# Dummy matmuls in the TensorE gaps of a planned attention and two-layer kernel

## The chip, the cores and the metric

One core of a Trainium2 chip runs the whole kernel. The metric is the device time of one execution in microseconds (us); lower is better. All times here are from three timed runs or from one profiled execution.

## The reference

Inputs: `q`, `k`, `v` of shape (4, 8, 576, 64) in float32, a scalar `tau`, and two pairs of weights, (512, 2048) and (2048, 512).

```python
scores = (q @ k.T) / sqrt(64)                       # per batch and head, 576 x 576
scores = where(scores >= max(scores, -1) - tau, scores, -1e9)
attn = exp(scores - max(scores, -1)); attn /= sum(attn, -1) + 1e-9
x = (attn @ v)                                      # heads side by side: 2304 x 512
h = x @ moe_w_in;  g = where(h >= 1, h, where(h <= -1, 0, (h + 1)**2 / 4)); x = g @ moe_w_out
h = x @ moe2_w_in; g = h - tanh(h);                 out = g @ moe2_w_out
```

## The kernel before

The attention is cut into 144 units of 128 query rows. A unit is a chain over four engines: `u_qk` (TensorE, PE) writes scores of 128 x 576 into a PSUM tile; `u_max` (VectorE, DVE) reads them for the row maximum; `u_exp` (ScalarE, ACT) reads them for the exponential; `u_mask` (DVE) reads them once more, compares them with the threshold and sums; then the rows are split in two halves of 16 bits, transposed and multiplied with `v`.

The scores lie in `s_ts[0]`, `s_ts[1]`, `s_ts[2]`. Each is one PSUM tile of 128 x 2 x 512 floats, so of two banks, and a unit uses columns 0 to 287 of both. The first 32 units (`N0`) take two or three of the tiles in turn. From then on every unit uses `s_ts[0]`, and the halves of the other two are the four accumulators `acc_ts` of the two feed-forward layers. Those layers run in 160 steps beside the units: `m_h` (matmuls into a tile `ph`), `m_act`, `m_dve`, `m_split`, `m_out` (matmuls into the accumulators) and, at the end of a layer, `m_evac`, which copies the accumulators out with ACT and DVE, one half tile after the other.

Every operation is first recorded by `Program.add` with an estimated duration. `Program.issue` then plays the program through as a list scheduler: each engine takes the ready operation of least `prio`, and `Program.run` gives its start and end. The instructions are emitted in the order of these planned starts, all engines in one list; the semaphores that order conflicting accesses of a tile are put in by the framework from that list. The planner's own dependences (`box`, `apart`) are finer: they compare the byte ranges.

`run` models the PE with two speeds: an operation takes `o.dur` when `self.warm` holds, else twice that. `run` also has a branch for fillers. It needs `self.filler`, which is set only when `FILL` holds, after all operations are recorded and before they are planned:

```python
out = s_ts[0][:, 1, HALF:512]
P.fill_bank = out.tensor.name, 1
P.filler = lambda: nc.tensor.matmul(out=out, lhsT=half_word[:, 0:128], rhs=half_word[:, 0:224], start=True, stop=True)
```

`half_word` is the float32 identity read as bf16. The output is columns 288 to 511 of the second bank of `s_ts[0]`, next to the scores. A planned operation carries the number of fillers in `o.fill`; `issue` emits them on the PE just ahead of it, unless an accumulation in that bank is open. Fillers are not operations of the plan, and nothing in the plan waits for them.

Of the kernel before, what the change touches and what calls it, by code (L numbers as in the profile page):

```python
# [46 lines left out]
LATENCY = {"PE": 55, "DVE": 34, "ACT": 34, "POOL": 78, "SP": 30}  # L47
DRAIN = 163
PATIENCE = 3.0
FILL = False  # L50
WINDOW = 3413.33
DIRECT = (3,)
NARROW = (0, 1)
# [109 lines left out]
class Program:  # L163
# [65 lines left out]
    def run(self, o, t):  # L229

        e = o.eng
        if e == "SP":
            turn = o.dur > 1000
            begin = max(self.dma, t + (1000 if turn else 900))
            self.dma = begin + o.serve
            self.free[e] = max(t + o.dur, begin - (2000 if turn else 4500)) + 60
            return t, self.dma + 1250
        if e == "PE":
            load, f0, f1 = self.load, self.free[e], t - 250
            fill = 0  # L240
            if self.filler and f0 > 6000 and t - f0 > 400:
                fill = int((f1 - f0) / 96)
                for k in range(int(f0 / WINDOW), int(f1 / WINDOW) + 1):
                    load[k] = load.get(k, 0.0) + max(min(f1, (k + 1) * WINDOW) - max(f0, k * WINDOW), 0.0)
            while self.slot < int(t / WINDOW):
                self.warm = load.get(self.slot, 0.0) > (0.4 if self.warm else 0.8) * WINDOW
                self.slot += 1
            d = o.dur * (1 if self.warm else 2)
            k = int(t / WINDOW)
            load[k] = load.get(k, 0.0) + min(t + d, (k + 1) * WINDOW) - t  # L250
            load[k + 1] = load.get(k + 1, 0.0) + max(t + d - (k + 1) * WINDOW, 0.0)
            self.free[e] = t + d
            o.fill = fill
            return t, t + d + DRAIN
        if o.lock:
            t = max(t, self.lock)
            self.lock = t + o.dur - OVERLAP[e]
        self.free[e] = t + o.dur - OVERLAP[e]
        return t, t + o.dur
# [73 lines left out]
def attention_moe_moe2(ctx: ExitStack, tc: tile.TileContext, qd, kd, vd, tau, w1, w2, ident, out):  # L333
# [711 lines left out]
    for k, _, fn, a in sorted(agenda, key=lambda e: e[:2]):  # L1045
# [3 lines left out]
        fn(*a)  # L1049
    if FILL:  # L1050
        half_word = idt.bitcast(BF16)
# [53 lines left out]
```

## Time and profile before

| | before |
|---|---|
| median of 3 runs | 1085.52 us (1084.07 to 1090.26) |
| the profiled execution, its own time | 1084.37 us |
| its span, first to last instruction | 1082.6 us |
| PE busy, instructions | 1030.0 us (95%), 5826 |
| DVE, ACT, POOL busy | 629.2, 632.4, 504.0 us |
| mean granted TensorE clock | 0.987 |

The busy time of the PE is made of matmuls whose ends are modelled, so it is not PE at its peak. The granted clock is a share of full speed: 1.00 is 2.4 GHz and 0.50 is 1.2 GHz.

### The profile page before, as it was taken

Reading aid. Unit: us, or ns where it says so; the run is one execution under the profiler, and the core shown is the slowest. Engines: PE = TensorE matmul, PEld = TensorE weight load, DVE = VectorE, ACT = ScalarE, POOL = GpSimd, SP = SyncE. Lnnn points to the kernel's source line nnn. Section 1 sums busy time; section 2 is a strip of 40 time slices with the busy share of each in tenths; the row PEclk is TensorE's granted clock in tenths of the full one; section 3 lists DMA queues with packets and bytes.
Section 4 is the critical chain, followed back from the end, with each engine's and each line's share of the span. In section 5 each row is a group of like instructions: output and inputs, shape, how many; then the busy total and the mean of one; then the engine's idle time right before and its main releaser. Section 6 shows DMA issues by size and latency. Waiting matters only on the chain.

```text
span 1082.6 us, 17257 instructions
## 1 busy us (share of the span) xinstructions
PE 1030.0 (95%) x5826; PEld 831.0 (77%) x5826; DVE 629.2 (58%) x1380; ACT 632.4 (58%) x1158; POOL 504.0 (47%) x510
## 2 busy tenths in 40 slices
PE   5789999999999999999999999999999999998997
PEld 3567777767777788778888888778877878888986
DVE  5987978898898766674347665742253331113432
ACT  5778777768776777676457777764353332222332
POOL 3654778768686555445345555444333212220000
PEclk8999999999999999999999999999999999999999
DMA  6999999999999998889679988897586655557997
GB/s 148 176 229 335 313 319 320 297 275 353 352 336 314 315 243 231 226 227 232 209 206 277 266 212 217 211 230 207 171 269 194 178 189 183 188 193 285 369 343 248
DMA packets 231384, 272.93 MB, mean 252 GB/s; under 512 B 170240, under 2 KB 170368, under 8 KB 231296
## 3 DMA queue, kind: packets, MB, share of 16 engines
q1 hardware_dynamic: 231296, 271.83, 86.5%
q8 instruction: 46, 0.75, 0.3%
q14 instruction: 42, 0.34, 0.1%
HBM read 193.40 MB, written 38.27 MB: 214 GB/s over the span
## 4 chain that ended last, share of the span: by engine, by line
PE 70%; DVE 12%; ACT 8%; DMA 5%; issue 4%; POOL 1%; SPq 0%; ACTq 0%; DVEq 0%; POOLq 0%
PE ph L354 35%; PE s L354 35%; DVE small L354 3%; DMA w<-in_w_dram 2%; ACT e L354 2%; DVE wr L354 2%; DVE e L354 2%; DMA vr<-in_vd_dram 2%; DVE g L354 1%; DVE xw L354 1%; ACT a L354 1%; DVE ph L354 1%; DMA wo<-wf0o 1%; ACT top L354 1%; DMA at<-w 1%
## 5 line engine op out<-in xcount | busy, mean ns | idle before, releaser
L354 PE MATMUL ph<-xh,wi 128*128 128x512 f32 x1024 | 271.1, 399 | 4.0 <-DVE g L354 3.7
L354 POOL TENSOR_TENSOR a<-e,a 128x512 f16<-128x512 f32 x236 | 180.9, 785 | 188.9 <-ACT a L354 172.4
L354 POOL TENSOR_TENSOR gl<-g,gh 128x512 fp32r<-128x512 f32 x114 | 152.3, 1336 | 199.1 <-ACT gh L354 179.4
L354 PEld LDWEIGHTS ph<-xh,wi 128*128 128x128 f32 x1024 | 188.0, 189 | 45.4 <-DVE g L354 6.2
L354 PE MATMUL s<-gh,wo 128*128 128x512 f32 (+1 forms) x640 | 157.4, 377 | 5.2 <-ACT gh L354 1.9
L354 PE MATMUL s<-wo,gh 128*128 128x512 f32 x576 | 155.1, 398 | 1.1 <-ACT w L354 0.7
L354 PE MATMUL ph<-xl,wi 128*128 128x512 f32 x512 | 144.8, 396 | 0.2 <-DVE xl L354 0.2
L354 DVE SCALAR_TENSOR_TENSOR e<-s,small,e 128x576 f32<-128x576 f32 x129 | 104.8, 813 | 67.1 <-ACT small L354 66.4
L354 DVE TENSOR_REDUCE small<-s 128x1 f32<-128x576 f32 x144 | 108.2, 752 | 47.7 <-PE s L354 46.8
L354 ACT ACTIVATE gh<-g 128x512 fp32r<-128x512 f32 (+1 forms) x152 | 88.2, 581 | 78.5 <-DVE g L354 76.2
L354 DVE TENSOR_TENSOR g<-ph,t 128x512 f32<-128x512 f32 (+1 forms) x80 | 50.8, 635 | 142.2 <-ACT t L354 138.9
L354 PEld LDWEIGHTS s<-gh,wo 128*128 128x128 f32 x640 | 112.0, 191 | 26.4 <-ACT gh L354 4.2
L354 PEld LDWEIGHTS s<-wo,gh 128*128 128x128 f32 x576 | 105.2, 188 | 22.9 <-ACT gh L354 1.1
L354 ACT ACTIVATE e<-s,small 128x576 f32<-128x576 f32 x129 | 94.9, 736 | 44.6 <-DVE small L354 41.7
L354 ACT ACTIVATE t<-ph 128x512 f32<-128x512 f32 (+1 forms) x80 | 44.1, 552 | 120.6 <-PE ph L354 120.4
L354 PEld LDWEIGHTS ph<-xl,wi 128*128 128x128 f32 x512 | 95.9, 188 | 23.2 <-DVE xl L354 1.2
L354 PE MATMUL s<-gl,wo 128*128 128x512 f32 (+1 forms) x320 | 89.4, 381 | 4.5 <-ACT xh L354 2.1
L354 DVE TENSOR_TENSOR ph<-ph,t 128x512 f32<-128x512 f32 (+1 forms) x80 | 51.4, 643 | 70.1 <-ACT t L354 69.2
L354 ACT ACTIVATE t<-ph,small 128x512 f32<-128x512 f32 (+1 forms) x80 | 51.4, 642 | 66.4 <-PE ph L354 66.2
L354 ACT ACTIVATE a<-e 128x576 f16<-128x576 f32 x118 | 80.1, 679 | 6.8 <-DVE e L354 4.8
L354 PE MATMUL s<-wo,gl 128*128 128x512 f32 x288 | 82.3, 393 | 1.0 <-ACT w L354 1.0
L354 PEld LDWEIGHTS s<-gl,wo 128*128 128x128 f32 x320 | 57.6, 190 | 15.8 <-ACT xh L354 3.4
(107 smaller groups left out, 1513.6 us busy)
## 6 DMA issues: line engine op xcount, KB each, us to landing
w<-in_w_dram SPq DMA_DIRECT2D x64, 512.0 KB, 6.0
wi<-wf0i SPq DMA_DIRECT2D x64, 512.0 KB, 4.1
wo<-wf0o SPq DMA_DIRECT2D x64, 512.0 KB, 4.3
wi<-wf1i SPq DMA_DIRECT2D x64, 512.0 KB, 3.8
wo<-wf1o SPq DMA_DIRECT2D x64, 512.0 KB, 3.7
kr<-in_kd_dram SPq DMA_DIRECT2D x32, 288.0 KB, 4.4
wf0i<-wi SPq DMA_DIRECT2D x16, 512.0 KB, 6.1
wf0o<-wo SPq DMA_DIRECT2D x16, 512.0 KB, 5.6
```

Source lines behind the costliest of these rows:

```text
L354: P.add(eng, dur, lambda: fn(**kw), outs, ins, serve, lock, load)
```

## The change

`FILL` becomes true. With the other edits, the planner gives a filler count to each PE operation before which its plan has the PE idle by more than 250 ns, from 3 us of planned time on: one filler for each 96 ns of the gap but its last 100 ns. The lines that counted fillers as activity in the planner's model of the clock go, so the planned starts, and with them the order of all other instructions, stay as they are.

```diff
-FILL = False
+FILL = True
...
         if e == "PE":
-            load, f0, f1 = self.load, self.free[e], t - 250
+            load, f0, f1 = self.load, self.free[e], t - 100
             fill = 0
-            if self.filler and f0 > 6000 and t - f0 > 400:
+            if self.filler and f0 > 3000 and t - f0 > 250:
                 fill = int((f1 - f0) / 96)
-                for k in range(int(f0 / WINDOW), int(f1 / WINDOW) + 1):
-                    load[k] = load.get(k, 0.0) + max(min(f1, (k + 1) * WINDOW) - max(f0, k * WINDOW), 0.0)
             while self.slot < int(t / WINDOW):
```

## Rows read from the trace of the kernel before

**Rows 1.** The page: busy time of engines, clock in 40 slices, chain by engine.
```profile
PE 1030.0 (95%) x5826; PEld 831.0 (77%) x5826; DVE 629.2 (58%) x1380; ACT 632.4 (58%) x1158; POOL 504.0 (47%) x510
...
PEclk8999999999999999999999999999999999999999
...
PE 70%; DVE 12%; ACT 8%; DMA 5%; issue 4%; POOL 1%; SPq 0%; ACTq 0%; DVEq 0%; POOLq 0%
```

**Rows 2.** Windows, four stages: us, busy us (x instructions) by engine, clock, DMA.
```profile
0.00:96.00 96.00, 73.47 (x589) 54.31 (x589) 75.19 (x223) 65.36 (x130) 49.87 (x69) 0.91 0.88 199
96.00:330.00 234.00, 220.95 (x1459) 173.90 (x1459) 199.13 (x401) 176.49 (x318) 177.05 (x154) 0.98 1.07 326
330.00:768.00 438.00, 432.85 (x2134) 348.74 (x2133) 255.73 (x559) 291.36 (x516) 219.55 (x237) 1.00 0.88 237
768.00:1082.60 314.60, 302.68 (x1649) 254.01 (x1647) 99.14 (x199) 99.21 (x195) 57.55 (x52) 1.00 0.70 235
```

**Rows 3.** Windows around four of the stretches at the lower clock.
```profile
13.00:21.00 8.00, 6.27 (x14) 3.77 (x14) 6.76 (x19) 5.66 (x13) 4.05 (x6) 0.57 0.31 70
...
109.00:113.00 4.00, 3.62 (x11) 2.79 (x12) 3.30 (x8) 2.72 (x5) 4.00 (x5) 0.57 1.28 352
156.00:161.00 5.00, 4.14 (x15) 3.71 (x16) 3.42 (x8) 2.28 (x5) 3.34 (x4) 0.66 1.05 295
207.00:212.00 5.00, 4.70 (x29) 3.80 (x30) 4.18 (x6) 4.23 (x7) 3.74 (x4) 0.66 1.17 269
```

**Rows 4.** Timeline of PE after eight gaps: start, us, what, [idle before, releaser].
```profile
70.90 0.84 PE L354 MATMUL s<-idt,e 128*128 128x128 f32 x5 [1.56 <-DVE e L354]
...
109.38 2.07 PE L354 MATMUL s<-gh,wo 128*128 128x512 f32 x4 [1.89 <-ACT gh L354]
...
156.86 1.65 PE L354 MATMUL ph<-xh,wi 128*128 128x512 f32 x3 [2.00 <-DVE g L354]
179.08 0.28 PE L354 MATMUL ph<-v,at 128*128 128x64 f16 x4 [0.50 <-DVE xw L354]
207.30 0.53 PE L354 MATMUL s<-kh,qtl 128*128 128x288 f32 x2 [1.96 <-DVE e L354]
...
226.10 1.20 PE L354 MATMUL s<-gl,wo 128*128 128x512 f32 x4 [0.78 <-DVE gl L354]
...
365.16 2.09 PE L354 MATMUL s<-gh,wo 128*128 128x512 f32 x8 [1.51 <-ACT v L354]
...
688.39 0.53 PE L354 MATMUL s<-kh,qs 128*128 128x288 f32 x2 [0.61 <-DVE e L354]
```

**Rows 5.** Timeline: the readers of the score tile nearest to five of those gaps.
```profile
107.91 0.72 ACT L354 ACTIVATE e<-s,small 128x576 f32<-128x576 f32 x1
...
156.72 0.81 DVE L354 SCALAR_TENSOR_TENSOR e<-s,small,e 128x576 f32<-128x576 f32 x1
...
206.42 0.82 DVE L354 SCALAR_TENSOR_TENSOR e<-s,small,e 128x576 f32<-128x576 f32 x1 [3.12 <-ACT small L354]
...
225.97 0.81 DVE L354 SCALAR_TENSOR_TENSOR e<-s,small,e 128x576 f32<-128x576 f32 x1
...
363.73 0.82 DVE L354 SCALAR_TENSOR_TENSOR e<-s,small,e 128x576 f32<-128x576 f32 x1 [1.19 <-ACT small L354]
```

**Rows 6.** Timeline at a layer's end: ACT empties `acc_ts[0]`, PE writes `acc_ts[1]`.
```profile
460.09 0.60 ACT L354 ACTIVATE xh<-s 128x512 fp32r<-128x512 f32 x1 [0.47 <-PE s L354]
460.74 0.19 PEld L354 LDWEIGHTS s<-gl,wo 128*128 128x128 f32 x1 [1.12 <-ACT xh L354]
460.74 0.50 PE L354 MATMUL s<-gl,wo 128*128 128x512 f32 x1 [0.69 <-ACT xh L354]
```

**Rows 7.** Timeline of PE: matmuls of 16 bits, and of 512 columns at either clock.
```profile
123.65 0.99 PE L354 MATMUL ph<-v,at 128*128 128x64 f16 x28
...
204.24 1.10 PE L354 MATMUL ph<-xl,wi 128*128 128x512 f32 x4
...
209.68 1.89 PE L354 MATMUL s<-gl,wo 128*128 128x512 f32 x4
...
507.77 1.26 PE L354 MATMUL ph<-at,v 128*128 128x288 f16 x9 [0.17 <-DVE g L354]
```

## The prediction

> **What bounds the kernel now.** Begin with the page: the PE is busy for 1030.0 of the 1082.6 us, and 70% of the chain that ended last runs through it [rows 1]. So there are 52.6 us of PE idle time in the span, and a change that touches only the PE can pay in two ways: by shortening work at the lower clock, or by moving gaps. Next, the same by stage [rows 2]. Before 96 us (attention alone) the PE idles 22.5 us, and the DVE, with 75.2 us, is as busy as the PE; 5.4 us of this idle time lie before the first matmul, where no filler goes. From 96 to 330 us (attention and the first layers) it idles 13.1 us, from 330 to 768 us 5.2 us, then 11.9 us. The last two stages hardly have a gap to fill.
>
> Then the clock. It is 0.91 in the first stage, 0.98 in the second and 1.00 after [rows 2]. At half speed, a mean of 0.91 over 96 us means 17 us at 1.2 GHz, and 0.98 over 234 us about 9 us; 0.987 over the whole span gives 28 us. These come in whole stretches: about 6.9 us between 13 and 21 us, and about 3.4 us each at 109, 156 and 207 us [rows 3]. The last three follow directly on the three longest gaps of the second stage, of 1.89, 2.00 and 1.96 us [rows 4]. In such a stretch four 512-column matmuls take 1.89 us, elsewhere 1.10 [rows 7]. If the PE were the only bound in all 28 us, the full clock would give back half, 14 us. That is the ceiling of what the change can win.
>
> **What a filler costs.** 28 matmuls of 64 columns of 16 bits pass in 0.99 us, 35 ns each with their weight loads; nine of 288 columns pass in 1.26 us, 140 ns each, both with the drain of the last one inside [rows 7]. A filler of 224 columns lies between; the planner counts 96 ns, which I take. At the lower clock it would be about twice that. A row of fillers is as long as the plan's gap less 0.1 us. The idle times shown begin at the modelled end of a matmul, some tenths of a microsecond after the slot that the planner counts, so I let the fillers of a gap last as long as the idle time shown. If the plan had just the gaps of the trace, that would be at most 47 us of fillers (52.6 less the 5.4 at the start), about 490. Where the gap is really there and the filler may start at once, it costs nothing: the PE's idle time is the cover. Where the PE arrives late, there is no gap and each filler is 0.1 us on the PE.
>
> **What a filler waits for** decides, I think. It writes into the second bank of `s_ts[0]`, beside the scores that `u_max`, `u_exp` and `u_mask` read. The planner's byte ranges don't overlap, but the semaphores go by something coarser. At 460 us the ACT empties the first accumulator from 460.09 to 460.69 us, and the PE, whose next matmul writes the second accumulator, the other half of the same tile, has its weight load held until 460.74 us, 0.69 us of idle matmul time released by that ACT instruction [rows 6]. There is no datum that passes between the two. So a filler waits for every reader of `s_ts[0]` that stands ahead of it in the list, and the matmul behind it waits with it, since the PE takes its instructions in order.
>
> The Trainium skill, page "PSUM — Partial Sum Buffer", section "PSUM bank collisions raise a hardware error", speaks against the change: it wants PSUM guarded by bank and quadrant and not by address, so unused columns of a bank in use are not free for the PE. By that rule a filler must not run beside a reader of the scores, which the wait just shown would see to; the sum below is what it comes to, against no wait and a gain of up to 14 us without it.
>
> A filler stands in the list just ahead of the operation that ends the gap, so all readers with a planned start before that are ahead of it. Take the gaps in turn, with the trace's times for the plan's. In each, the cost is the reader's end plus the fillers' time, less the moment at which the PE resumed before [rows 4, 5].
>
> - 207.30 us: the PE waits for the mask (206.42 to 207.24 us) itself, since the next unit needs the tile. The fillers wait for the same mask and run only after it: 1.96 us lost, and the idle time in front, with the fall of the clock, stays.
> - 156.86 us: the PE is released by the DVE's `g`, and the mask starts 0.14 us before the PE resumes. Fillers wait for its end at 157.53 and then take 2.0 us: 2.7 us.
> - 109.38 us: the exponential ends at 108.63; 1.9 us of fillers end at 110.5: 1.15 us. Here the PE's idle time shrinks from 1.89 to about 1.1 us, which may save this fall of the clock: 3.4 us at half speed, so 1.7 us back.
> - 226.10 us: mask until 226.78, then 0.8 us: 1.5 us.
> - 365.16 us: mask until 364.55, then 1.5 us: 0.9 us.
> - Twelve further gaps of 0.25 to 0.79 us between 96 and 768 us (the first shown is at 179, the last at 688 us) hold 5.8 us of idle time. Five of them end with a mask, most others have a reader in flight. At about the gap's own length each: 5 us; none if no reader were in flight.
> - 70.90 us, in the first stage: the next transpose needs the mask, and from there to 82 us the chain runs on the PE: 1.6 us.
>
> This makes 14.8 us. For the rest of the first stage I take a gain: the gap ahead of 13 us lies after the exponential and ahead of the mask of its unit, so its fillers can run at once, and part of the 6.9 us at the lower clock behind it (at most 3.4 us) comes back; I take 2 us. The other delays there hit the PE while the DVE has work waiting, and I take them as nothing; that cover is gone wherever all three score tiles are empty, and then each costs about its gap, in all up to some 10 us. With the 1.7 us at 109 us the sum is 14.8 - 1.7 - 2 = 11 us.
>
> Of this I take three quarters, 8 us. The plan need not have the gaps of the trace: some of these are surprises to it, as the wait at 460 us, which its byte ranges don't contain, and there no filler stands. A PE that comes later also finds its next operand ready sooner. The profiled execution took 1084.4 us, 0.1% below the median of the runs, so 8 us more than the median is 1093.5 us. What is late next, after a held PE, is the following unit's `u_max` and the `m_act` of the running step; late readers also wait for fillers that stand ahead of them.
>
> **The rivals.** Half a per cent, 5.4 us, is about what a measurement of this kernel tells from no change.
>
> 1. *The gaps are filled at once and the clock stays up*: faster. This decides if the readers are mostly done or not yet in the list when a gap opens. For it speaks that nearly all the time at half speed lies in two stages with known gaps, and that three stretches follow on gaps of 2 us. Against it speak the readers in flight in all five long gaps shown. If two thirds of the 14 us come back at a cost of 1 us: 1085.5 - 8 = 1077 us. Chance 0.16. The Trainium skill, "TensorE: Matmul & The Clock Gate", section "What's actually happening", says that the low clock is the default and that activity releases it. By that rule, fillers that run would bring this time; by the rows, most can't run in the gap.
> 2. *Little happens*: the plan has few gaps beyond the first 96 us, or the fillers fall away since an accumulation is open in that bank, or gain and cost are alike: 1080 to 1091 us, about 1086. Chance 0.22.
> 3. *Far more fillers than real gaps*: the plan sees the PE idle where it is behind in fact, or the DVE runs dry in the first stage. With all 47 us of fillers at half cover, 23 us: 1109 us; for it speaks only that the plan isn't shown. Chance 0.12.
>
> My forecast, fillers held by readers at 5.5 to 18 us, so 1091 to 1104 us, has 0.50.
>
> **How the numbers follow.** Slower by over 0.5% holds the forecast and rival 3: 0.62. Within 0.5%: 0.22. Faster: 0.16. The range reaches into rival 1 and through half of rival 3: 1079 to 1109 us, leaving about 0.1 on either side. The likeliest case's own range is 1091 to 1104.
>
> **What would show it.** In the profile after: a few hundred more PE instructions that write `s` from the identity; among the PE's waits, the readers of the score tile (DVE `e`, DVE `small` and ACT `e`) as releasers of these fillers; at about 157 and 207 us PE idle time ahead of the fillers, and the matmuls behind them later after their own operand. The clock near 15 us should be higher than 0.57, at 207 us still low. Wrong would be: fillers that start right at a gap's opening with no wait (rival 1, clock near 1.00 from 96 us on); fewer than 150 of them (rival 2); or fillers where the PE was not idle before (rival 3).

## The result and the profile after

The changed kernel takes 1099.24 us (median of 8 runs, 1094.28 to 1101.96), the kernel before 1087.11 us in the same comparison (8 runs): a ratio of 1.0101, 95% interval 1.0074 to 1.0129. It is slower by about 1%, some 11 us. The profiled execution took 1100.13 us, with a span of 1098.3 us.

The lines of its page that answer to [rows 1]:

```profile
PE 1043.9 (95%) x5983; PEld 845.4 (77%) x5983; DVE 630.4 (57%) x1380; ACT 633.1 (58%) x1158; POOL 505.8 (46%) x510
...
PEclk8998999999999999999999999999989999999999
...
PE 69%; DVE 10%; ACT 7%; DMA 6%; issue 4%; POOL 2%; SPq 1%; ACTq 0%; DVEq 0%; POOLq 0%
```

There are 157 more matmuls, far fewer than the 490 that the trace's idle time allowed. (The plan gives 167 fillers to 28 gaps. Ten of them stand where an accumulation in their bank is open, and `issue` leaves these out; 157 in 25 rows are emitted, 20 of these rows in the first stage.) The PE's busy time grew by 13.9 us and the span by 15.7, so the idle time did not shrink: it is 54.4 us now, after 52.6. Next the windows by stage, as in [rows 2]:

```profile
0.00:96.00 96.00, 74.57 (x674) 57.79 (x675) 73.06 (x216) 61.99 (x123) 47.69 (x67) 0.96 0.83 184
96.00:330.00 234.00, 221.56 (x1473) 176.05 (x1473) 195.09 (x400) 176.41 (x318) 174.46 (x152) 0.98 1.06 323
330.00:768.00 438.00, 430.99 (x2138) 346.76 (x2137) 261.64 (x565) 293.03 (x519) 224.31 (x239) 1.00 0.91 237
768.00:1098.30 330.30, 316.78 (x1704) 264.82 (x1702) 100.57 (x201) 101.71 (x199) 59.36 (x53) 0.99 0.69 230
```

In the first 96 us the clock rose from 0.91 to 0.96, yet the other engines did less there: the DVE has 216 instructions behind it instead of 223, the ACT 123 instead of 130. The stage fell behind although its matmuls ran faster. The group of the fillers (count; busy us; mean ns of one, which is long since neighbours overlap; then the PE's idle time before them with its releasers):

```profile
L1052 PE MATMUL s<-idt 128*128 128x224 bf16 x157 | 19.8, 264 | 16.4 <-DVE e L352 4.1 <-ACT e L352 3.1 <-DVE wr L352 2.9
```

And from the list of waits, those between the fillers and the readers of the score tile (total us, times, longest):

```profile
PE s L1052 <- DVE e L352: 4.1, 4, 1.6
ACT wr L352 <- PE s L1052: 3.6, 3, 1.7
PE s L1052 <- ACT e L352: 3.1, 4, 0.9
PE s L1052 <- DVE wr L352: 2.9, 2, 2.0
PE s L1052 <- DVE small L352: 2.5, 3, 0.8
PE s L1052 <- ACT wr L352: 2.4, 1, 2.4
DVE wr L352 <- PE s L1052: 1.9, 1, 1.9
```

The masks and exponentials write `e` or, for the early units, a spare buffer `wr`; `small` is the row maximum. Of the 16.4 us of idle time ahead of fillers most ends with such a reader, and readers wait for fillers in turn. Three places in the timeline of the changed kernel show what that does. At the gap that was at 70.90 us in [rows 4]:

```profile
75.55 0.81 DVE L352 SCALAR_TENSOR_TENSOR e<-s,small,e 128x576 f32<-128x576 f32 x1
...
76.43 1.50 PE L1052 MATMUL s<-idt 128*128 128x224 bf16 x14 [1.65 <-DVE e L352]
77.77 0.71 PE L352 MATMUL s<-idt,e 128*128 128x128 f32 x5
```

The transpose used to start 0.86 us after its mask began (70.04 to 70.90). Now the mask begins at 75.55, the idle time of 1.65 us is as long as before, and the 14 fillers come on top: 2.22 us from mask to transpose, 1.36 us lost. The longest row of fillers in the first stage:

```profile
42.19 0.74 ACT L352 ACTIVATE wr<-s,small 128x576 f32<-128x576 f32 x1 [2.23 <-DVE small L352]
42.81 0.81 DVE L352 SCALAR_TENSOR_TENSOR wr<-s,small,wr 128x576 f32<-128x576 f32 x1
42.98 2.46 PE L1052 MATMUL s<-idt 128*128 128x224 bf16 x24 [2.40 <-ACT wr L352]
45.28 1.63 PE L352 MATMUL s<-kr,g 128*128 128x288 f32 x6
45.58 0.82 DVE L352 SCALAR_TENSOR_TENSOR wr<-s,small,wr 128x576 f32<-128x576 f32 x1 [1.89 <-PE s L1052]
```

The PE idles 2.40 us until the exponential is through, then runs 24 fillers, 96 ns from one to the next; the scores of the next unit start 2.3 us after the first filler, and a mask that needs nothing from these fillers waits 1.89 us for them. And the first layer's gap, at 109.38 us before:

```profile
115.14 0.74 ACT L352 ACTIVATE e<-s,small 128x576 f32<-128x576 f32 x1
115.93 2.36 PE L1052 MATMUL s<-idt 128*128 128x224 bf16 x23 [0.92 <-ACT e L352]
115.97 0.62 ACT L352 ACTIVATE gh<-g 128x512 fp32r<-128x512 f32 x1
118.07 1.18 PE L352 MATMUL s<-gh,wo 128*128 128x512 f32 x4
```

Its operand `gh` is there at 116.59 us and the matmul starts at 118.07: 1.4 us lost. The clock, 0.57 behind this gap in [rows 3], is 1.00 there now (second line), but a new fall stands ahead of the gap (first line), where before has 0.88 in the same 8 us:

```profile
103.00:111.00 8.00, 7.48 (x25) 6.41 (x26) 3.72 (x6) 4.76 (x9) 1.41 (x1) 0.57 1.02 416
116.00:120.00 4.00, 4.00 (x32) 3.58 (x32) 3.13 (x6) 3.04 (x6) 3.93 (x3) 1.00 1.01 288
```

From 84 to 132 us the mean clock is 0.93 in both profiles, so nothing was won here.

### The profile page after: what moved, and what is told of

Its sections match the earlier page's. It is cut to its first block, busy times and chain, and to the rows that moved or that the text cites. A ratio compares the mean times of both kernels' runs of the same rounds, so it can differ in the third digit from the quotient of the medians.

```text
span 1098.3 us, 17570 instructions
## 1 busy us (share of the span) xinstructions
PE 1043.9 (95%) x5983; PEld 845.4 (77%) x5983; DVE 630.4 (57%) x1380; ACT 633.1 (58%) x1158; POOL 505.8 (46%) x510
## 4 chain that ended last, share of the span: by engine, by line
PE 69%; DVE 10%; ACT 7%; DMA 6%; issue 4%; POOL 2%; SPq 1%; ACTq 0%; DVEq 0%; POOLq 0%
PE ph L352 34%; PE s L352 34%; DVE small L352 3%; DMA w<-in_w_dram 2%; ACT e L352 2%; DMA vr<-in_vd_dram 2%; DVE e L352 2%; DVE wr L352 1%; PE s L1052 1%; DMA wo<-wf0o 1%; DVE g L352 1%; DVE xw L352 1%; DMA wi<-wf1i 1%; SPq L352 1%; DVE ph L352 1%
## 5 line engine op out<-in xcount | busy, mean ns | idle before, releaser
L352 DVE TENSOR_REDUCE small<-s 128x1 f32<-128x576 f32 x144 | 108.4, 753 | 52.6 <-PE s L352 51.6
```

Of the source, the lines that this page charges most:

```text
L352: P.add(eng, dur, lambda: fn(**kw), outs, ins, serve, lock, load)
```

## The experiments

Theory A, of the prediction: what costs is that a filler shares the score tile, so it is held until a reader is through and then stands in front of the matmul that the reader releases too. Theory B: the fillers' own time on the PE costs, wherever they write. Theory C: the growth behind 330 us, where no filler stands, is an effect of the change. Each kernel is the changed one but for the edit shown, and its ratio is to the kernel before on the same chip.

**One part alone: the first stage, and the rest.**

```diff
-            if self.filler and f0 > 3000 and t - f0 > 250:
+            if self.filler and 3000 < f0 < 85000 and t - f0 > 250:    # early
+            if self.filler and f0 > 85000 and t - f0 > 250:           # late
```

> Fillers only in the gaps that the plan has before 85 us (125 of the 167, 23 of the 28 groups); the order of all else is unchanged. Held by readers: the units of the first stage are pushed back, the shift of the row maxima against the kernel before is about +5 us by the 30th unit as in the changed kernel, the time some 4 to 6 us above before. Filler time alone: 125 of 167, three quarters of the 12 us, +9 us. Later shift by transfers: the growth behind 330 us, where no filler stands, comes again (+7 us), so +12 us in all.

> Fillers only in the five gaps that the plan has after 85 us (42 of the 167). Held by readers: the group of 23 ahead of the first layer waits for an exponential and costs about 2 us at 110 us, of which the stretch at half speed behind 157 us may give back as much; within 2 us of before. Filler time alone: a quarter of the 12 us, +3 us. Later shift by transfers: +7 us.

Measured: early 1095.04 us against 1086.33 us, ratio 1.0085 (1.0059 to 1.0112); late 1089.94 us, 1.0021 (0.9994 to 1.0049). The loss is made in the first stage, about 9 us of it; what the 42 later fillers do can't be told from nothing. Early is nearer to B's number than to A's, so B was still open.

**One filler per gap.**

```diff
-                fill = int((f1 - f0) / 96)
+                fill = 1
```

> One filler per gap instead of up to 24: 28 in all, 2.7 us of matmul time, but each still waits for the readers of the score tile ahead of it. Held by readers: the waits stay, at least half of the loss remains, +5 to +8 us (the clock gains nothing, since nothing is filled). Filler time alone: 28 of 167, +2 us. Later shift by transfers: +7 us or nothing, by whether it hangs on the exact times.

Measured: 1090.22 us, ratio 1.0026 (1.0001 to 1.0050), 2.8 us. Its group:

```profile
L1052 PE MATMUL s<-idt 128*128 128x224 bf16 x25 | 7.0, 280 | 15.3 <-DVE e L352 4.7 <-ACT e L352 2.5 <-DVE small L352 2.4
```

My expectation for A was wrong, and B's +2 us came out: with the waits kept (15.3 us) and the rows of fillers cut, most of the loss goes. So the waiting alone is not what costs. My reading is that it ends with the same reader that would have held the next matmul anyway, as at 70.90 us, and that what adds is the row of fillers behind it.

**Fillers only behind the last reader.** The list is followed while it is emitted, and a gap is filled only from the planned end of the last reader that stands ahead.

```diff
...
+            if o.eng != "PE" and self.fill_bank and self.fill_bank[0] in o.names:
+                read = max(read, o.avail + 60)
             if o.eng == "PE":
+                if o.fill:
+                    f0, f1 = o.open
+                    o.fill = max(int((f1 - max(f0, read)) / 96), 0)
...
```

> A filler is put into a gap only from the planned end of the last reader of the score tile that stands ahead of it in the list: 33 fillers in 10 groups are left. Held by readers: little is waited for, within 2 us of before. Filler time alone: 33 of 167, +2.4 us. Later shift by transfers: +7 us or nothing.

Measured: 1086.17 us, ratio 1.0000 (0.9975 to 1.0025). No loss is measured, though B's +2.4 us lies just inside the interval too. Of the 33 fillers left, 23 are emitted, in 7 of the 25 rows: in most of the gaps a reader is, by the plan, at work up to the gap's end.

**The same load on the PE without the PSUM.**

```diff
-        P.filler = lambda: nc.tensor.matmul(out=out, lhsT=half_word[:, 0:128], rhs=half_word[:, 0:224], start=True, stop=True)
+        P.filler = lambda: nc.tensor.ldweights(half_word[:, 0:128])
```

> Each filler is only a load of the identity as weights, with no matmul behind it: as many fillers in the same places, on the PE about as long (98 ns each in the changed kernel's trace), but they write no PSUM and so wait for no reader. Held by readers: they run while the gap is open, the loss goes, within 3 us of before. Filler time alone: 167 times 0.1 us on the PE as in the changed kernel, +12 us. If loads alone also keep the clock up, a little below before (up to -3 us).

Measured: 1086.89 us against 1087.32 us, ratio 1.0003 (0.9976 to 1.0030). Its group in the profile:

```profile
L1052 PEld LDWEIGHTS <-idt 128*128 128x128 bf16 x157 | 7.8, 97 | 2.5 <-DVE wr L352 0.8 <-issue 0.8
```

The waits are gone (2.5 us of idle time before them, for 16.4), and no loss is measured. But the loads took 7.8 us of the engine, not the 15 or 16 of the matmuls, so B is weakened and not out: half its 12 us would be 6. The mean clock of the 12 runs was 0.987, that of before 0.986: loads alone did not keep it up.

**The same fillers, earlier in the list.** They are emitted at the planned start of the gap, not at its end.

```diff
...
+            while gaps and (o.start >= gaps[0].gap or o is gaps[0]):
+                g = gaps.pop(0)
+                if not opened.get(self.fill_bank):
+                    for _ in range(g.fill):
+                        self.filler()
...
```

> The same 167 matmul fillers, in the same order on the PE, but they stand in the list where the plan's gap opens instead of just ahead of the operation that closes it: readers of the score tile that start within the gap now come behind them. Held by readers: fewer waits ahead of the fillers, instead some masks and exponentials wait for fillers; at most half of the 12 us is left, +2 to +6 us. Filler time alone: +12 us.

Measured: 1096.92 us, ratio 1.0081 (1.0052 to 1.0111). The expectation failed: the fillers wait far less, but 9 us are lost all the same. Its group of fillers, and three of its waits:

```profile
L1057 PE MATMUL s<-idt 128*128 128x224 bf16 x157 | 19.9, 266 | 4.9 <-ACT e L357 2.2 <-DVE e L357 1.0 <-DVE wr L357 0.8
```

```profile
DVE small L357 <- PE s L1057: 4.6, 4, 2.2
ACT e L357 <- PE s L1057: 3.3, 2, 2.7
PE s L1057 <- ACT e L357: 2.2, 3, 1.3
```

The coupling turned round: the readers now wait for the fillers, as at the row of 24, where a row maximum waits for it to be over, 2.3 us after the matmuls ahead of the fillers ended (first line):

```profile
41.42 1.22 PE L357 MATMUL s<-kr,g 128*128 128x288 f32 x4
42.47 2.46 PE L1057 MATMUL s<-idt 128*128 128x224 bf16 x24
44.97 0.76 DVE L357 TENSOR_REDUCE small<-s 128x1 f32<-128x576 f32 x1 [1.49 <-PE s L1057]
```

That fits A if the tile is what couples, and B if the PE's time is. So the tile itself had to be taken away.

**The same fillers into a tile that nobody reads.** In these three kernels the first stage uses two score tiles, so the third is free until 70 us of the plan, and only gaps before 58 us are filled, with 150 fillers. The last two differ in one index.

```diff
-        st = s_ts[0 if i >= N0 else i % (2 if len(DIRECT) and i >= 8 * min(DIRECT) else 3)]
+        st = s_ts[0 if i >= N0 else i % 2]
...
-            if self.filler and f0 > 3000 and t - f0 > 250:
+            if self.filler and 3000 < f0 < LAST and t - f0 > 250:     # LAST = 58000; FILL is false in two_none
...
-        out = s_ts[0][:, 1, HALF:512]
+        out = s_ts[2][:, 1, HALF:512]                                 # two_apart alone
```

> All units of the first stage use two score tiles in turn instead of three, so that the third is free until the direct units transpose into it (70 us in the plan). No fillers. A base for the next two: slower than before by 5 to 20 us, since a unit waits for the tile of the one two ahead.

> The same with two score tiles, and 150 matmul fillers in the plan's gaps before 58 us, written beside the scores of the first tile as in the changed kernel. Held by the score tile: +6 to +12 us against the base with two tiles. Filler time alone: 150 times 96 ns, of which the changed kernel lost three quarters, +10 us.

> The same 150 fillers in the same places of the list, all else the same, but written into the third tile, which no other instruction touches before 70 us. Held by the score tile: no wait either way, the fillers run while the gaps are open, within 3 us of the base with two tiles or below it by what the clock gives. Filler time alone: +10 us as with the shared tile.

Measured, against 1087.03 us of before: no fillers 1103.17 us (1.0141, 1.0113 to 1.0169), shared tile 1113.34 us (1.0228, 1.0197 to 1.0259), own tile 1104.01 us (1.0162, 1.0128 to 1.0197). The same 150 matmuls in the same places cost 10.2 us (1113.34 - 1103.17) beside the scores and 0.8 us, less than these intervals can tell from nothing, in a tile of their own. Their groups, shared first:

```profile
L1053 PE MATMUL s<-idt 128*128 128x224 bf16 x150 | 18.6, 272 | 14.5 <-DVE wr L353 7.5 <-DVE e L353 5.9 <-ACT wr L353 0.6
```

```profile
L1053 PE MATMUL s<-idt 128*128 128x224 bf16 x150 | 17.3, 259 | 0.0
```

In a tile of their own they never wait. B forecast +10 us there, so B falls, and that the shared tile is what costs is shown. The difference is clear, though the runs spread: 1105.83 to 1114.75 us shared, 1100.14 to 1109.68 us apart. Of the 10.2 us the clock can account for 3 at most: by their granted clocks, the runs with the shared tile were at half speed for 26.3 us, those without fillers for 20.4.

Two things this pair does not show. One is the direction of the coupling: at the opening the fillers waited little, and the loss was much the same. The other is whether it goes by tile or by bank, since the third tile lies in other banks too. For the tile speaks [rows 6], where the two accumulators are different banks of one tile.

**Once more before and after, for their profiles.**

> The kernel before once more, for its profile: which part of the shift behind 330 us, where no filler stands, is a matter of the execution. If it is the execution: steps of 1 to 5 us against the first profile of before at the same places (behind 365 and 800 us). If the fillers cause them: none there.

> The changed kernel once more, for its profile: the shift up to the first layer (+7 us) should come again by either theory; the 5 us at 800 us only if the fillers cause them.

Measured: 1085.88 and 1097.24 us. In every kernel here but those with two score tiles the same row maxima follow in the same order, so the start of the n-th can be compared over the profiles. The 7th, 33rd, 48th and 144th start at 22.7, 102.0, 193.5 and 851.7 us in the first profile of before; the table has how much more time the others took between them, worked out from these starts in each trace.

| profile | 7th to 33rd | 33rd to 48th | 48th to 144th |
|---|---|---|---|
| before, again | +2.1 us | -2.5 us | +5.1 us |
| after | +6.2 | -2.0 | +10.2 |
| after, again | +9.9 | +0.4 | +5.5 |
| early | +9.8 | -1.6 | +4.9 |
| late | +0.3 | -1.3 | +12.9 |
| one filler per gap | +7.0 | -1.5 | +3.5 |
| fit | +3.8 | +0.1 | +2.8 |
| weights | -1.1 | -1.6 | +6.6 |
| at the opening | +6.9 | +1.2 | +3.2 |

In the first column the kernels with the early fillers stand apart by 4 to 8 us from before, again. In the last one they don't: before itself took 5.1 us more the second time, and the most, 12.9, stands with late, whose profiled execution was 4.3 us above its median. Of the single step of 5.1 us near 800 us in the first profile of after, 2.7 us are a load of `vr` that took 8.31 us, and the rest is the clock behind the wait for it, which takes the next eight matmuls from 2.12 to 3.78 us,

```profile
803.41 8.31 DMA vr<-in_vd_dram
...
814.61 3.78 PE L352 MATMUL ph<-xh,wi 128*128 128x512 f32 x8 [3.38 <-DVE g L352]
```

where the same piece of the chain of before reads

```profile
792.77 5.63 DMA vr<-in_vd_dram
...
801.29 2.12 PE L354 MATMUL ph<-xh,wi 128*128 128x512 f32 x8 [0.69 <-DVE g L354]
```

and in the second profile of after the steps there took 0.6 us less than in the first of before. So C has no support: a single profile of a kernel like this carries 5 us and more of its execution's own.

## Why the prediction was right

The direction and the size (8 us forecast, some 11 to 12 measured) held, and so did the heart of the mechanism: sharing the score tile is what costs. That the size came so near is luck, since two large terms were wrong in opposite directions. By its steps:

- *A filler waits for readers of the score tile, though it touches none of their bytes.* Right, and shown: 14.5 us of idle time ahead of the 150 fillers that share the tile, none ahead of the same 150 in their own. The wait at 460 us [rows 6] was the evidence for it, before a single filler existed. The wait is not all that costs: at the opening it was 4.9 us, and about 9 us were lost.
- *At each gap, the fillers' time is added behind the reader.* Right at the two filled gaps that can be compared. At 70.90 us the sum had 1.6 us and the trace shows 1.36; at 109.38 us it had 1.15 and the trace shows 1.4.
- *The plan's gaps are those of the trace.* This step failed. Of the five long gaps between 96 and 400 us only the one at 109.38 us exists in the plan. The terms for 156.86, 207.30, 226.10 and 365.16 us (7.1 us) and for most of the twelve small gaps (5 us) are void: late shows +2.3 us with an interval that reaches below zero. The discount of a quarter for this was much too small: without these terms the sum of 14.8 us, less the 3.7 us for the clock, is about -1 us.
- *The other delays of the first stage are nothing, since the DVE has work waiting.* This term was mis-sized the other way: 20 of the 25 rows of fillers stand there, and early cost 9 us. The prediction named the cover and the price if it was gone (up to 10 us), and took the wrong end. The two errors nearly cancel in the sum.
- *The fillers ahead of 13 us can run at once.* This failed. No filler stands in the gap that ended at 13.62 us before; the first row, at 14.01 us, waits 1.12 us for a mask, and from 13 to 21 us the clock is 0.63 where it was 0.57.
- *The clock gives something back, much less than 14 us.* Right for the whole. Over the 8 runs of after the mean clock is 0.988, over 35 of before 0.986: 25.6 against 29.9 us at half speed per run, so some 2 us gained at half price, where the sum had 3.7. By place it is not shown. The fall behind 109 us is gone in late, which has this row of fillers and comes out of it at the shift it had before (0.87 us ahead of the first profile of before at its 33rd row maximum, 0.86 at its 40th). But both profiles of after fall at about 104 us instead, and the second profile of before, without a filler, has its fall at 96 us and 1.00 from 104 to 132 us.
- *Against rival 1*: where fillers could run at once (their own tile) nothing was lost, but nothing measurable was won either. The Trainium skill's rule that activity releases the low clock ("TensorE: Matmul & The Clock Gate", section "What's actually happening") agrees with the first stage, where the mean clock is 0.96 in both profiles of after and was 0.91 and 0.93 in those of before. It did not decide the time. The Trainium skill's rule to guard PSUM by bank and not by address ("PSUM — Partial Sum Buffer", section "PSUM bank collisions raise a hardware error") agrees with the 14.5 us of waits at disjoint columns of one bank; the wait at 460 us, between two banks of one tile, goes beyond it.

Not settled: how the 9 us of the first stage divide between matmuls that start late and readers that start late. At the opening and at the close of the gap the loss was nearly the same.

## What to carry to other kernels

A dummy instruction is free only if it shares nothing with the work that the gap is waiting for: look at what its output and its inputs are tied to before counting its time. A gap on an engine that takes its instructions in order is often somebody else's instruction at work, and here that instruction was mostly reading the very tile the filler wrote. Ask too whether the gaps that a planner sees are those of the trace; here they shared only one of the five long ones behind 96 us.

## What was not expected

150 matmuls of 224 columns in 16 bits ran in the gaps of the first stage at no measurable cost once they had a tile of their own (1104.01 against 1103.17 us). And 157 loads of 128 x 128 weights in 16 bits had no measurable cost either (ratio 1.0003, 0.9976 to 1.0030), yet left the mean clock where it was (0.987 against 0.986).
